# Four edits in the backward half of an H3 convolution and gated MLP kernel: late transposes, an eviction moved to VectorE, two more banks, earlier weights

## The chip, the cores and the metric

The kernel runs on one core of one Trainium2 chip. Its time is the device time of one execution, in microseconds (us). The core has TensorE (PE; PEld is its weight load), VectorE (DVE), ScalarE (ACT), GpSimd (POOL) and SyncE (SP). SP, ACT and POOL also issue the DMA transfers, each from a queue of its own, in order.

## The reference

The reference computes one forward pass and all its gradients for a sequence of 2048 positions and 1024 channels.

```python
xn = layernorm(q)                          # 2048 x 1024
ks = shift convolution of k, four taps per channel (shift_k)
kv = ks * v
y  = long causal convolution of kv with ssm_k (2048 taps per channel, by FFT) + kv * ssm_D
s  = xn * y
g  = silu( ((xn @ w_gate) * (xn @ w_up)) @ w_down )      # 3584 inner columns
out = q + s * g
return out, gradients for q, k, v, shift_k, ssm_k, ssm_D, w_gate, w_up, w_down
```

All inputs and outputs are bf16.

## The kernel before, in words

Everything is done in one program, in four stages, each of which TensorE fills with large products while the convolution's work is slipped in between.

1. **Forward products** (to 568 us). `gu_unit` multiplies the normalised input with slabs of w_up and w_gate (L463), writes both results and their product to DRAM (GUTd, HTd). In between a generator, `conv_forward`, does the shift and the long convolution as short Fourier transforms by matmul and products on VectorE.
2. **Down product and gate** (573 to 787 us). `bm_mm` (L813) multiplies with w_down, held in the tiles U0 to U6. `gate` (from L816) forms the output and the gradients that start the backward pass: dbm, its transposed form DBMT (tiles U7 to U10), and dy, stored to DYd. Its pools `mh`, `mi`, `mt` and `mo` are released at the end of the stage, and only then the pool `bw` is made, which holds the transposed weights wdt.
3. **Backward slabs** (793 to 1852 us). There are 14 slabs of 256 inner columns. `load_wdt` brings a slab of w_down transposed by DMA, on SP's queue. `dh_half` loads the stored gate and up values (tile gul, four buffers), forms two products of eight matmuls each (L915, PSUM psdh), which ScalarE evicts to dht (L917), and multiplies gul by dht on VectorE. Its function `turn` then stores gul to DGUTd and transposes it on TensorE through the one PSUM bank `ps_tr` (L930), from which ScalarE copies it to a tile U4, U5 or U6 (L931). `dw_slab` multiplies the stored input with these for the gradients of w_gate and w_up (L938, PSUM psdw, evicted as wb at L942). One half slab `dh_slab_half(sl + 1, 0)` is done ahead of `dw_slab(sl)`. After the 14 slabs `dwd_slab` forms the gradient of w_down (L1007) and, near the end, weights for the last stage are transposed (L997).
4. **Input gradient** (from 1852 us). `dx_part` (L1063) and `ln_backward`.

**When a turn runs.** `defer` puts a turn on a list; each `flush(age)` adds one to the age of all that is listed and runs those of at least that age. `dh_half` flushes once per product, so twice, and `dw_slab` flushes once for each of its eight columns.

**When the convolution's work runs.** `conv_backward` is a generator whose `yield` values are estimates of VectorE's work. `btick(n)` adds to a counter and lets `bpump` run the generator up to the same share of `C_TOTAL`. It does the transforms of dy for the eight blocks of 128 channels (`dy_forward`, the tiles dyx and kvx, PSUM psS and psP from the pool `ps_c3` and psY from `ps_y`, one bank each). Then come 16 units: eight for the gradients of k and v, eight for that of ssm_k. Each unit is a `product` of two spectra A and B on VectorE and a first part of the inverse transform, `inv_dft` (tile W, written back into B); its rest, the `tail`, is run between the steps of the next unit. For ssm_k the tail is `dh_tail`: four times 16 small matmuls from B into psY (L755), which ScalarE scales and writes into the tile ho in order of time (L758). In ho the eight residues of a position lie next to each other, so that one eviction writes values 16 bytes apart. Last come eight `dk_unit`s, for the gradient of k (tile dka, one buffer) and of shift_k: 16 matmuls into psY (L791), of which VectorE takes diagonals (tile dt2, L795).

All small VectorE operations go through a helper at L182, all loads of `ld` through L61 (SP), stores through `st` at L64 (POOL) and `sta` at L67 (ACT). A scheduler orders the instructions of each engine from the program's order and its priorities when the kernel is built; each engine then runs them strictly in that order.

Of the kernel before, what the change touches and what calls it, by code (L numbers as in the profile page):

```python
# [10 lines left out]
ACT = mybir.ActivationFunctionType  # L11
ALU = mybir.AluOpType
AX = mybir.AxisListType
BF16 = mybir.dt.bfloat16
F32 = mybir.dt.float32
# [4 lines left out]
def build_kernel(  # L20
# [11 lines left out]
    nc = tc.nc  # L32
    P = 128
# [4 lines left out]
    DC = D // P  # L38
    NF = F // P
    SLW = 256  # L40
    NSL = F // SLW
    EPS = 1e-5
    WSC = 2.0 / 2048.0
# [14 lines left out]
    V = nc.vector  # L58

    def ld(out, in_):  # L60
        return nc.sync.dma_start(out=out, in_=in_)  # L61

    def st(out, in_):
        return nc.gpsimd.dma_start(out=out, in_=in_)  # L64
# [15 lines left out]
    def pool(name, bufs=1, side=None, space=None):  # L80
        kw = dict(name=name, bufs=bufs, reuse_waits="tile")
        if side:
            kw["side"] = side
        if space is not None:
            kw["space"] = space
        return tc.alloc_tile_pool(**kw)
# [94 lines left out]
    def tt(o, a, b, op):  # L181
        V.tensor_tensor(o, a, b, op)  # L182

    ADD, SUB, MUL = ALU.add, ALU.subtract, ALU.mult
# [36 lines left out]
    FWD4_W = 2 * (2 * 1.5 + 2.8)  # L221
# [48 lines left out]
    PROD_W = 14.0  # L270
# [29 lines left out]
    INV_W = 2.3 + 2.4 + 2.3 + 2.8  # L300

    def gseg(G, r, j, k):
        a = r % 4
        return G[:, 4 * a + 2 * j + (1 - k if a == 3 else k), :]
# [74 lines left out]
    ps_y = pool("ps_y", 1, space=PSUM)  # L379
# [63 lines left out]
    def defer(fn):  # L443
        later.append([0, fn])

    def flush(age=0):

        for e in later:
            e[0] += 1
        while later and later[0][0] >= age:  # L450
            later.pop(0)[1]()
# [166 lines left out]

    ub = pool("ub", 1, side="right")
    U += [ub.tile([P, 4096], BF16, name=f"U{i}") for i in range(4, 11)]  # L620
    mh = pool("mh", 2, side="right")
    mi = pool("mi", 2, side="right")
    mt = pool("mt", 1, side="right")
# [121 lines left out]
    def dh_tail(ds, G, ew):  # L745
        ho = ew.tile([P, 2, P, 8], BF16, name="ho")
        for c in range(2):
            for rq in range(2):
                ps = ps_y.tile([P, 4, P], F32, name="psY")
                for i in range(4):  # L750
                    r = 4 * rq + i
                    n = 0
                    for j in range(2):
                        for k in range(2):
                            nc.tensor.matmul(ps[:, i, :], gseg(G, r, j, k)[:, c * P:(c + 1) * P], TI[:, j, r, k, :],  # L755
                                             start=(n == 0), stop=(n == 3))
                            n += 1
                nc.scalar.activation(ho[:, c].rearrange("p u r -> p r u")[:, 4 * rq:4 * rq + 4], ps[:], ACT.Copy, scale=WSC)  # L758
                yield 0.1
        st(o_dssmk[ds * P:(ds + 1) * P, :], ho[:].rearrange("p c u r -> p (c u r)"))  # L760
        yield 0.1

# [11 lines left out]
    def dk_unit(ds, tiles, ew):  # L774
        dsl = slice(ds * P, (ds + 1) * P)
        kh, dk = tiles
        acc = ew.tile([P, 2, 8, P], BF16, name="dka")
        wb = lambda j: Wbc[:, j:j + 1, dsl].to_broadcast([P, 8, P])
        for c in range(2):
            tt(acc[:, c], dk[:, c, 3:11, :], wb(3), MUL)  # L780
            for j in (2, 1, 0):
                prod = ew.tile([P, 8, P], BF16, name="dkp")
                tt(prod[:], dk[:, c, j:j + 8, :], wb(j), MUL)
                tt(acc[:, c], acc[:, c], prod[:], ADD)
                yield 1.6
            st(o_dk[:, c, :, dsl], acc[:, c])
        ps = ps_y.tile([P, 4, P], F32, name="psY")
        n = 0
        for c in range(2):
            for r in range(8):  # L790
                nc.tensor.matmul(ps[:].rearrange("p a b -> p (a b)"), dk[:, c, r, :],  # L791
                                 kh[:, c, r:r + 4, :].rearrange("p a b -> p (a b)"), start=(n == 0), stop=(n == 15))
                n += 1
        dt_ = ew.tile([P, 4, P], F32, name="dt2")
        tt(dt_[:], ps[:], ident_f[:].unsqueeze(1).to_broadcast([P, 4, P]), MUL)  # L795
        dr_ = ew.tile([P, 4], F32, name="dr2")
        V.tensor_reduce(dr_[:], dt_[:], AX.X, ADD)
        V.tensor_copy(dsko[:, ds, ::-1], dr_[:])
        yield 1.5

    C_TOTAL = 8 * (FWD4_W + 0.8) + 16 * (PROD_W + INV_W) + 8 * 1.4 + 8 * 5.4 + 8 * 0.5 + 8 * 11.2
    bpump, bdrain = make_pump(conv_backward(), C_TOTAL)

    ddo = const.tile([P, 8], BF16, name="ddo")
# [6 lines left out]
    def bm_mm(ps, ht, i, fc):  # L811
        for dh in range(2):
            nc.tensor.matmul(ps[:, dh * 512:(dh + 1) * 512], ht[:, fc, i * P:(i + 1) * P],  # L813
                             WD[fc // 4][:, fc % 4, dh * 512:(dh + 1) * 512], start=(fc == 0), stop=(fc == NF - 1))
# [39 lines left out]
    def load_ht(bp):  # L854
        ht = mh.tile([P, NF, 256], BF16, name="ht")
        ld(ht[:], HTd[:, bp * 256:(bp + 1) * 256].rearrange("(c f) s -> f c s", f=P))
        return ht

    ht = mh.tile([P, NF, 256], BF16, name="ht")
    for j in range(7):  # L860
        if j % 2 == 0:
# [8 lines left out]
        gate(i, pss[i])  # L870
    for bp in range(1, 8):
        ht = load_ht(bp)
        for i in range(2):
            ps = ps_bm.tile([P, D], F32, name="psbm")
            for fc in range(NF):
                bm_mm(ps, ht, i, fc)
                if fc == 14:
                    flush()
            gate(2 * bp + i, ps)
# [4 lines left out]


    XN = [u8(q, a=4) for q in range(4)]
    bw = pool("bw", 2, side="right")
    bg = pool("bg", 2, side="right")
    ps_dh = pool("ps_dh", 2, space=PSUM)
    ps_dw = pool("ps_dw", 2, space=PSUM)  # L890
# [1 line left out]
    ps_c3 = pool("ps_c3", 1, space=PSUM)  # L892
    ps_y = pool("ps_y3", 1, space=PSUM)
    bcnt = [0]
    BT = 0.94 * (NSL * (8 + 16) + 7 * 16.0)

    def btick(n):
        bcnt[0] += n
        bpump(bcnt[0] / BT)

    def load_wdt(sl):
        wdt = bw.tile([P, DC, SLW], BF16, name="wdt")
        nc.sync.dma_start_transpose(out=wdt[:], in_=B_w_down[sl * SLW:(sl + 1) * SLW, :])
        return wdt

    def dh_half(fc, hf, wdt, dgu):

        fi = fc % 2
        gut = bg.tile([P, 2, 1024], BF16, name="gul", bufs=4)
        ld(gut[:], GUTd[fc, :, :, hf * 1024:(hf + 1) * 1024])  # L910
        dht = bg.tile([P, 1024], BF16, name="dht")
        for k in range(2):
            ps = ps_dh.tile([P, 512], F32, name="psdh")
            for dc in range(DC):
                nc.tensor.matmul(ps[:], wdt[:, dc, fi * P:(fi + 1) * P], DBMT[2 * hf + k][:, dc, :],  # L915
                                 start=(dc == 0), stop=(dc == DC - 1))
            nc.scalar.copy(out=dht[:, k * 512:(k + 1) * 512], in_=ps[:])  # L917
            flush(2)
            btick(1)
        dgt = gut  # L920
        with tc.high_priority(60):
            tt(dgt[:], gut[:], dht[:].unsqueeze(1).to_broadcast([P, 2, 1024]), MUL)

        def turn():
            sta(DGUTd[4 * hf:4 * hf + 4, :, :, fc, :].rearrange("b f a s -> f a b s"),
                dgt[:].rearrange("f a (b s) -> f a b s", s=256))
            for a in range(2):
                ps = ps_tr.tile([P, 8, P], BF16, name="tr")
                for i in range(8):
                    nc.tensor.transpose(ps[:, i, :], dgt[:, a, i * P:(i + 1) * P], ident[:])  # L930
                nc.scalar.copy(out=dgu[:, :, a, fi * P:(fi + 1) * P], in_=ps[:])  # L931
        defer(turn)

    def dw_slab(sl, dgus):
        for dc in range(DC):
            ps = ps_dw.tile([P, 2, SLW], F32, name="psdw")
            for b in range(NB):
                nc.tensor.matmul(ps[:].rearrange("p a f -> p (a f)"), XN[b // 4][:, b % 4, dc * P:(dc + 1) * P],  # L938
                                 dgus[b // 8][:, b % 8].rearrange("p a f -> p (a f)"),
                                 start=(b == 0), stop=(b == NB - 1))  # L940
            wb = bg.tile([P, 2, SLW], BF16, name="wb", bufs=4)
            nc.scalar.copy(out=wb[:], in_=ps[:])  # L942
            fs = slice(sl * SLW, (sl + 1) * SLW)
            sta(o_dwg[dc * P:(dc + 1) * P, fs], wb[:, 0, :])
            sta(o_dwu[dc * P:(dc + 1) * P, fs], wb[:, 1, :])
            flush(2)
            btick(2)

    def load_h(sp):
# [1 line left out]
        nc.sync.dma_start_transpose(out=h, in_=HTd[sp * SLW:(sp + 1) * SLW, :])  # L951
        return h

    wdt = load_wdt(0)
    flush()
    def dh_slab_half(sl, hf, wdt):
        dgu = u8(4 + (2 * sl + hf) % 3, "p (b a f) -> p b a f", b=8, a=2)
# [6 lines left out]
    for sl in range(NSL):  # L964
# [13 lines left out]
        wdt = wnext  # L978
# [124 lines left out]
    for bp in range(1, 8):  # L1103
        t = load_dgut(bp)
        for i in range(2):
            ps = ps_x.tile([P, D], F32, name="psx")
# [68 lines left out]
```

## Time and profile before

| | |
|---|---|
| median of three runs | 2256.11 us (2255.44 to 2267.16) |
| profiled execution | 2267.18 us, its span 2265.1 us |
| busy share of the span | TensorE 94%, VectorE 58%, ScalarE 34%, GpSimd 12% |
| granted TensorE clock, mean | 0.984 |
| DMA | 436.92 MB, mean 193 GB/s |

The span runs from the first to the last instruction of the program; 2.1 us of the execution lie outside of it. A matmul's busy time is its time in a pipeline, so that a busy share near 100% does not say that the array is fully used; waits and the granted clock say where time is lost. "A <- B" in the views of waits reads "A waited until B was done".

### The profile page before, as it was taken

The numbers are of one execution on the slowest core, as the hardware profiler recorded it, in microseconds if no ns is written. First come the engines' busy times: TensorE is split into PE (matmuls) and PEld (weight loads), VectorE is DVE, ScalarE is ACT, GpSimd is POOL, SyncE is SP. The second block draws the span as 40 slices with busy tenths as digits, with TensorE's granted clock in tenths as the row PEclk, the third lists the DMA queues.
The fourth block names the chain that finished last, engine by engine and source line by source line (L and its number), as shares of the span: only waits on it lengthen the run. The fifth ranks groups of instructions, "written<-read, shape, count | busy, mean of one in ns | idle before, by whom it ended". The sixth has DMA issues, their size and how long they took to land.

```text
span 2265.1 us, 29905 instructions
## 1 busy us (share of the span) xinstructions
PE 2122.9 (94%) x12128; PEld 1096.0 (48%) x12128; DVE 1311.4 (58%) x1770; ACT 769.3 (34%) x1040; POOL 273.8 (12%) x440
## 2 busy tenths in 40 slices
PE   5899999999899889989999999988998999999997
PEld 3455555555344455544545545444443455444443
DVE  8779898987354555659775676674456202222122
ACT  4433434343233343333333335554411242111111
POOL 3211111111021110011211200000021000000000
PEclk9999999999999999999999999999999999999999
DMA  9646565555977786686886755546688865323221
GB/s 312 232 175 231 190 207 196 189 174 188 323 233 231 246 263 198 167 258 200 251 211 209 226 163 168 177 160 188 138 240 146 235 216 173 135 107 117 103 107 33
DMA packets 386795, 436.92 MB, mean 193 GB/s; under 512 B 120960, under 2 KB 304280, under 8 KB 375520
## 3 DMA queue, kind: packets, MB, share of 16 engines
q1 hardware_dynamic: 227664, 177.23, 27.7%
q0 software_dynamic: 40944, 175.96, 22.5%
q10 hardware_dynamic: 118048, 81.81, 12.4%
q8 instruction: 95, 1.56, 0.3%
q14 instruction: 44, 0.36, 0.0%
HBM read 237.76 MB, written 179.34 MB: 184 GB/s over the span
## 4 chain that ended last, share of the span: by engine, by line
issue 27%; PE 21%; DVE 7%; ACT 4%; DMA 4%; POOL 1%; ACTq 1%; POOLq 0%; DVEq 0%
PE psdw L938 11%; PE psdw L1007 3%; DVE m L182 3%; PE psdh L915 3%; ACT ho L758 2%; ACT U L931 1%; PE tr L930 1%; DVE gul L182 1%; ACTq L67 1%; PE psY L755 1%; PE psY L314 1%; DMA DYFd<-DX 1%; DVE A L182 1%; POOL out_dram L64 1%; DVE W L182 1%
## 5 line engine op out<-in xcount | busy, mean ns | idle before, releaser
L463 PE MATMUL psg<-U,wslab 128*128 128x512 bf16 x1792 | 407.5, 383 | 9.2 <-ACT gut L465 5.6
L938 PE MATMUL psdw<-U,U 128*128 128x512 bf16 x1792 | 408.0, 382 | 1.3 <-ACT wb L942 1.3
L1063 PE MATMUL psx<-U,dgut 128*128 128x512 bf16 x1408 | 308.5, 379 | 0.0
L463 PEld LDWEIGHTS <-wslab 128*128 128x128 bf16 x1792 | 176.3, 99 | 208.4 <-issue 17.2
L1063 PEld LDWEIGHTS <-dgut 128*128 128x128 bf16 x1792 | 174.7, 98 | 208.1
L938 PEld LDWEIGHTS <-U 128*128 128x128 bf16 x1792 | 174.1, 99 | 193.9 <-issue 6.9
L465 ACT CAST gut<-psg 128x512 bf16<-128x512 f32 x224 | 130.9, 585 | 269.7 <-PE psg L463 252.0
L915 PE MATMUL psdh<-U,wdt 128*128 128x512 bf16 x896 | 213.4, 385 | 6.7 <-DMA wdt<-in_B_w_down_dram 6.7
L813 PE MATMUL psbm<-U,ht 128*128 128x512 bf16 x896 | 199.4, 383 | 10.0 <-DMA ht<-HTd 10.0
L1007 PE MATMUL psdw<-U,U 128*128 128x512 bf16 x896 | 201.6, 381 | 0.0
L182 DVE TENSOR_TENSOR m<-A,B 128x1024 bf16<-128x1024 bf16 (+1 forms) x160 | 116.7, 792 | 92.7 <-DMA B<-KFd 72.0
L942 ACT CAST wb<-psdw 128x512 bf16<-128x512 f32 x112 | 66.5, 594 | 249.8 <-PE psdw L938 213.3
L182 DVE TENSOR_TENSOR dxn<-psx,dxna_t 128x1024 f32<-128x1024 f32 x16 | 19.6, 1224 | 220.8 <-PE psx L1063 220.7
L813 PEld LDWEIGHTS <-ht 128*128 128x128 bf16 x896 | 87.8, 99 | 115.0 <-DMA ht<-HTd 11.0
L931 ACT COPY U<-tr 128x1024 bf16<-128x1024 bf16 x112 | 114.2, 1019 | 59.5 <-PE tr L930 38.0
L1007 PEld LDWEIGHTS <-U 128*128 128x128 bf16 x896 | 86.5, 98 | 98.4 <-issue 1.7
L915 PEld LDWEIGHTS <-wdt 128*128 128x128 bf16 x896 | 86.5, 99 | 95.7 <-DMA wdt<-in_B_w_down_dram 7.2
L182 DVE TENSOR_TENSOR W<-W,psP 128x512 f32<-128x512 f32 x128 | 81.6, 683 | 63.7 <-ACT W L214 54.0
L1079 ACT ACTIVATE junk<-dxn 128x1024 bf16<-128x1024 f32 x16 | 16.9, 1057 | 279.8 <-DVE dxn L182 279.8
L917 ACT CAST dht<-psdh 128x512 bf16<-128x512 f32 x112 | 68.8, 615 | 93.0 <-PE psdh L915 70.0
L182 DVE TENSOR_TENSOR gul<-gul,dht 128x2048 bf16<-128x2048 bf16 x56 | 68.4, 1221 | 53.4 <-ACT dht L917 48.1
L930 PE MATMUL tr<-ident,gul 128*128 128x128 bf16 x896 | 69.5, 221 | 26.6 <-ACT U L931 13.1
(220 smaller groups left out, 2520.5 us busy)
## 6 DMA issues: line engine op xcount, KB each, us to landing
gul<-GUTd SPq DMA_DIRECT2D x56, 512.0 KB, 5.9
DGUTd<-gul ACTq DMA_DIRECT2D x56, 512.0 KB, 5.9
dgut<-DGUTd SPq DMA_DIRECT2D x16, 1792.0 KB, 8.3
GUTd<-gut ACTq DMA_DIRECT2D x48, 512.0 KB, 3.9
A<-DYFd POOLq DMA_DIRECT2D x16, 1024.0 KB, 5.8
out_dram<-wb ACTq DMA_DIRECT2D x224, 64.0 KB, 2.4
ht<-HTd SPq DMA_DIRECT2D x7, 1792.0 KB, 8.3
HTd<-hT POOLq DMA_DIRECT2D x48, 256.0 KB, 3.4
```

The costliest lines, as they stand in the source:

```text
L182: V.tensor_tensor(o, a, b, op)
L463: nc.tensor.matmul(ps[:], w[:, dc, a, fi * P:(fi + 1) * P], XNT[q][:, dc, :], start=(dc == 0), stop=(dc == DC - 1))
L465: nc.scalar.copy(out=gut[:, a, k * 512:(k + 1) * 512], in_=ps[:])
L813: nc.tensor.matmul(ps[:, dh * 512:(dh + 1) * 512], ht[:, fc, i * P:(i + 1) * P], WD[fc // 4][:, fc % 4, dh * 512:(dh + 1) * 512], start=(f ...
L915: nc.tensor.matmul(ps[:], wdt[:, dc, fi * P:(fi + 1) * P], DBMT[2 * hf + k][:, dc, :], start=(dc == 0), stop=(dc == DC - 1))
L917: nc.scalar.copy(out=dht[:, k * 512:(k + 1) * 512], in_=ps[:])
L930: nc.tensor.transpose(ps[:, i, :], dgt[:, a, i * P:(i + 1) * P], ident[:])
L931: nc.scalar.copy(out=dgu[:, :, a, fi * P:(fi + 1) * P], in_=ps[:])
L938: nc.tensor.matmul(ps[:].rearrange("p a f -> p (a f)"), XN[b // 4][:, b % 4, dc * P:(dc + 1) * P], dgus[b // 8][:, b % 8].rearrange("p a f ...
L942: nc.scalar.copy(out=wb[:], in_=ps[:])
L1007: nc.tensor.matmul(ps[:], h[:, b, fi * P:(fi + 1) * P], DBM[b // 4][:, b % 4, dh * 512:(dh + 1) * 512], start=(b == 0), stop=(b == NB - 1))
L1063: nc.tensor.matmul(ps[:, dh * 512:(dh + 1) * 512], t[a][:, 4 * j + f, i * P:(i + 1) * P], WGU[n][:, f, dh * 512:(dh + 1) * 512], start=(n ...
```

## The change

There are four edits and what belongs to them.

- A turn is run once its age is 4 in `dh_half` and 3 in `dw_slab`, in place of 2 in both.
- The eviction of psY into ho is a VectorE operation in place of a ScalarE activation. The work that `dh_tail` announces to the pump rises with it, and `C_TOTAL` too.
- `dk_unit` takes psS and psP from `ps_c3` in turn in place of psY, and dka has two buffers.
- The pool `bw` is made ahead of the pools of the second stage, and the first slab of wdt is loaded in that stage's loop (at bp == 5). The pump does nothing for the first eight ticks of the slabs, and its share is counted from there.

```diff
     ub = pool("ub", 1, side="right")
     U += [ub.tile([P, 4096], BF16, name=f"U{i}") for i in range(4, 11)]
+    bw = pool("bw", 2, side="right")
...
-                nc.scalar.activation(ho[:, c].rearrange("p u r -> p r u")[:, 4 * rq:4 * rq + 4], ps[:], ACT.Copy, scale=WSC)
-                yield 0.1
+                V.tensor_scalar(ho[:, c].rearrange("p u r -> p r u")[:, 4 * rq:4 * rq + 4], ps[:], WSC, None, op0=MUL)
+                yield 0.7
...
-        acc = ew.tile([P, 2, 8, P], BF16, name="dka")
+        acc = ew.tile([P, 2, 8, P], BF16, name="dka", bufs=2)
...
-        ps = ps_y.tile([P, 4, P], F32, name="psY")
+        ps = ps_c3.tile([P, 4, P], F32, name=("psS", "psP")[ds % 2])
...
-    C_TOTAL = 8 * (FWD4_W + 0.8) + 16 * (PROD_W + INV_W) + 8 * 1.4 + 8 * 5.4 + 8 * 0.5 + 8 * 11.2
+    C_TOTAL = 8 * (FWD4_W + 0.8) + 16 * (PROD_W + INV_W) + 8 * 1.4 + 8 * 5.4 + 8 * 2.9 + 8 * 11.2
...
+    def load_wdt(sl):
+        wdt = bw.tile([P, DC, SLW], BF16, name="wdt")
+        nc.sync.dma_start_transpose(out=wdt[:], in_=B_w_down[sl * SLW:(sl + 1) * SLW, :])
+        return wdt
...
         ht = load_ht(bp)
+        if bp == 5:
+            wdt = load_wdt(0)
...
-    bw = pool("bw", 2, side="right")
...
-        bpump(bcnt[0] / BT)
-
-    def load_wdt(sl):
-        wdt = bw.tile([P, DC, SLW], BF16, name="wdt")
-        nc.sync.dma_start_transpose(out=wdt[:], in_=B_w_down[sl * SLW:(sl + 1) * SLW, :])
-        return wdt
+        bpump((bcnt[0] - 8) / (BT - 8))
...
             nc.scalar.copy(out=dht[:, k * 512:(k + 1) * 512], in_=ps[:])
-            flush(2)
+            flush(4)
             btick(1)
...
             sta(o_dwu[dc * P:(dc + 1) * P, fs], wb[:, 1, :])
-            flush(2)
+            flush(3)
             btick(2)
...
-    wdt = load_wdt(0)
     flush()
```

## The prediction

> **What bounds the kernel now.** I read the page's engine line first, then its slices, then the waits of TensorE stretch by stretch, because a sum over the whole span hides which engine is late where.
>
> ```profile
> PE 2122.9 (94%) x12128; PEld 1096.0 (48%) x12128; DVE 1311.4 (58%) x1770; ACT 769.3 (34%) x1040; POOL 273.8 (12%) x440
> PEclk9999999999999999999999999999999999999999
> ```
>
> TensorE is busy 94% of the span and no other engine passes 58%, so time goes away only where TensorE stands idle or runs below its clock. The change leaves its 12128 matmuls and transposes as they are. The next view is TensorE's waits from 787 to 1580 us (the slabs of the gate, up and inner gradients), then from 1580 to 1850 us (the down gradient). Columns: who waited, for whom, total us, times, longest.
>
> ```profile
> PE psY L755 <- ACT ho L758: 14.7, 8, 5.8
> PE tr L930 <- ACT U L931: 13.1, 11, 3.7
> PE tr L930 <- DVE gul L182: 11.6, 5, 4.6
> PE psdh L915 <- DMA wdt<-in_B_w_down_dram: 6.7, 1, 6.7
> PE psY L646 <- DMA dyx<-DYd: 3.7, 1, 3.7
> ...
> PE psY L791 <- DVE dt L182: 6.7, 2, 6.2
> PE psY L755 <- ACT ho L758: 5.1, 3, 1.8
> PE tr L997 <- DMA wn<-in_B_w_up_dram: 4.8, 1, 4.8
> PE psY L791 <- DMA dkh<-DKSHd: 2.7, 1, 2.7
> ```
>
> Each of the four edits is aimed at a line of this list. Their cost is more than the waits, since the clock drops after the long ones. The table by stretches has, near its end, the granted clock; these rows surround the waits for wdt, for two gul products, for ho and for dt.
>
> ```profile
> 790.00:800.00 10.00, 6.37 (x25) 2.97 (x26) 4.82 (x8) 1.61 (x3) 3.60 (x6) 0.66 1.06 303
> 1000.00:1060.00 60.00, 55.36 (x316) 28.82 (x317) 54.77 (x60) 21.29 (x31) 8.53 (x13) 0.94 0.71 205
> 1540.00:1560.00 20.00, 13.92 (x94) 7.93 (x92) 18.54 (x24) 9.21 (x8) 0.00 (x0) 0.83 0.58 206
> 1645.00:1660.00 15.00, 12.27 (x50) 5.07 (x49) 8.29 (x14) 1.17 (x2) 5.01 (x9) 0.89 1.08 313
> 1735.00:1755.00 20.00, 13.81 (x53) 5.64 (x52) 16.04 (x26) 1.17 (x2) 4.75 (x7) 0.83 0.62 160
> ```
>
> Length times the missing share is the time lost: 3.4, 3.6, 3.4, 1.7 and 3.4 us.
>
> [...] a wait of 6.7 us is followed by the 0.66 above, and waits of 1.8 us are followed by nothing. [...] The tile ho is written 16 bytes apart, and there ScalarE takes 2452 ns for 128x512, against 586 ns for the packed yl of the same size: [...] no row shows VectorE writing so. [...] the nearest row, DX<-W at 128x512 out of f32, is 685 ns. I use 685.
>
> ```profile
> L758 ACT ACTIVATE ho<-psY x32: 2433/2452/2524, 1361.9 to 1641.0; 128x512 bf16<-128x512 f32 x32
> L732 ACT CAST yl<-psY x32: 585/586/606, 1021.6 to 1335.9; 128x512 bf16<-128x512 f32 x32
> L182 DVE TENSOR_TENSOR DX<-W 128x512 bf16<-128x512 f32 x64 | 40.2, 685 | 3.5 <-DMA DYFd<-DX 3.5
> ```
>
> **The change part by part.**
>
> *Early down weights.* Where instructions stand I take from the order of the changed program as it is built, which holds no times. There both first transposes of w_down, slabs 0 and 1, stand on SP directly behind the last weight slabs and ahead of the first load into U, so they are issued near 493 us and not at 786.9. Being issued that early, they are moved past every load of the middle stage. They now wait for the last KSHd store (443.7) and the last kv product (446.1), both done. SP issues nothing from 493 to 532 us, where its next load waits for TensorE, and the two took 6.4 us to issue: that stretch hides them. Were it gone, the U loads would be 6.4 us later and TensorE would start L813 that much later. Gone are the 6.7 us wait and 3.4 us of clock. The gul loads, which stood behind the transposes on SP (793.5), follow the U loads near 782 to 787. What is late next: dyx is read after DYd of the last gate is stored (issued 792.0) and landed at 805.3, while the new order has TensorE there near 802; I count 1 us of gain. Sum 11, between 6 and 14.
>
> *Transposes four products late.* A turn now stands 4 products (4 x 1.72 us) behind its own product instead of 2, so a late gul may be 3.4 us later for free; the longest of the five waits is 4.6. Gain 11.6, and 3.6 of clock. The 13.1 us on U are another matter: there is one transpose bank, and the second transpose stands 5 matmuls (1.08 us) behind the first while the copy takes 1.02 and its latency; two of the eleven, 6.7 us, came while ScalarE was held up issuing wb stores for 6.4 and 2.6 us. I expect 3 us back here, as ScalarE loses the ho work. New: the second turn of a half slab comes right ahead of the column that reads it. The order leaves 2.1 to 2.4 us from its last transpose to that read, and copy plus latency need about 1.3, more if ScalarE is in a dht eviction (0.6). 14 slabs by 0.2 us is 3, between 0 and 10. gul has four buffers and three are now held at once; the next load has the 27 us of a dw_slab to land, so nothing. Sum 11.6 + 3.6 + 3 - 3 = 15, between 5 and 20.
>
> *ho by VectorE.* Removed: 14.7 + 5.1 = 19.8 us and 3.4 of clock. Added: 32 x 0.685 = 22 us on VectorE, which is idle over a third of 1280 to 1580 us. Its order decides, for psY has one bank: a group of 16 transposing matmuls can't start before the previous ho is out, and in the new order ho stands behind parts of the next unit's inverse. Walked for one unit from the durations of the trace: last psY of the old unit at 0; B lands 7 us later; product and turn 12.4 + 1.3; W 2.3, B 2.4, W 2.3, B 1.2, then ho at 29.0. TensorE, without waits, has the first psY group done at 23.8 and wants the second at 27.3; it starts at 29.9 and waits 2.6. Walked so, the eight units wait about 2, 3.7, 2.4, 2.5, 2.6, 3.1, 1.5 and 0.6: 18 us, of which I take 16, for groups that move past one another. [...] At 2452 ns instead of 685, 1.8 us more for each unit, 14, and 9 of clock. Sum 19.8 + 3.4 - 16 - 3.4 = 4, between -19 and +23. What queues behind a waiting ho on VectorE are the next product and gul, the first of which waits for B anyhow.
>
> *Two banks for the shift product.* psS and psP lie idle by then. The 6.7 us behind dt go, with 3.4 of clock. The order has 52 instead of 36 matmuls (3.4 us) ahead of the first shift product, which covers the 2.7 us for dkh and 1.7 of clock. Sum 14, between 9 and 15. The second dka buffer ends 26.8 us of VectorE's waits for stores, off the path: nothing.
>
> *Pacing.* The side work starts 8 ticks later, runs 5% faster per tick (647.2 / 413.1 against 628 / 421.1) and ends on the same tick; VectorE keeps a slack of some 4 us per unit. Nothing, at worst -4.
>
> Together 11 + 15 + 4 + 14 = 44. The profiled execution took 2267.2 us, so 2223 by this sum. The median of the three runs is 2256.1, 11 below it; some of the waits above must be missing there, so I take 40 off the median: **2216 us**.
>
> **The rivals.**
>
> *Slow scattered writes.* VectorE pays as ScalarE does. For: the same addresses. Against: nothing shown. 23 us of the gain go: 2239, still faster.
>
> *The transposes change their waiter.* The one transpose bank and ScalarE's stalled issues, not gul, end every wait at L930, and the late copies cost their 10; the ho waits reach 18 to 25. For: ACT U has the largest count. Against: the five gul waits are separate lines. The turn is -5, ho -10, so 11 - 5 - 10 + 14 = 10 off: 2246 to 2252, no measurable change.
>
> *VectorE becomes the bound.* If each of the 24 later psY groups finds a half inverse (2.3 + 2.4) ahead of its ho, and ho costs 2.45, with 3.45 us of products between groups, each waits 3.7: 88 us. Less 20 saved there and 40 elsewhere it is 28 slower, 2284, and up to 41 more if each drops the clock, 2325. It decides from 2.5 us per group. For: one bank and a queue in order. Against: VectorE waits for B 72 us in this part, and the walk finds only one long wait per unit.
>
> **How the numbers follow.** Forecast 60%, slow writes 19%, changed waiter 10%, VectorE the bound 11%. A measurement of this kernel tells about 0.5%, 11 us, from no change: faster 0.79, same 0.10, slower 0.11. The low end takes most of the good bounds of ho, turns and start (19 + 5 + 3 more), 24: 2192. The high end takes in slow writes and the third case: 2254. Left out are the fourth case and a little below the low end.
>
> **What would show it.** Right: no wait of TensorE for wdt; clock 1.00 after 790; no wait of L930 for gul over 1 us; none for dt; ho on VectorE near 0.7 us; waits of psY for ho of 2 to 4 us, one per unit. Wrong: ho near 2.4 us; waits of psY that sum over 40 us; waits of L938 for U at each slab.

## The result, and the profile after

The changed kernel is slower: 2286.13 us median of four runs (2283.51 to 2297.08) against 2256.07 us, a ratio of 1.0131 with a 95% interval of 1.0085 to 1.0177. The profiled execution took 2297.08 us, its span 2295.2 us, which is 30.1 us more than the span before. The mean granted clock fell from 0.984 to 0.977 of full speed; the missing shares times the spans are 36 and 53 us, so by this estimate up to 17 of the 30 us are clock and at least 13 are waits. TensorE's busy time, for the same matmuls, grew by 8.9 us (2131.8 against 2122.9) and its idle time by 21, which puts less on the clock and more on the waits.

The first two lines are the engine line and TensorE's clock row of the page.

```profile
PE 2131.8 (93%) x12128; PEld 1097.0 (48%) x12128; DVE 1387.5 (60%) x1802; ACT 694.2 (30%) x1008; POOL 273.6 (12%) x440
PEclk9999999999999999999999999999999899999999
```

VectorE has 76 us more to do and ScalarE 75 us less. The 32 operations that moved are as long on the one engine as on the other, 2432 ns on VectorE against 2452 on ScalarE. This row is from the view of the tile ho in the changed kernel (shortest, middle and longest in ns, then first and last start in us):

```profile
L759 DVE TENSOR_SCALAR ho<-psY x32: 2409/2432/2449, 1363.9 to 1664.8; 128x512 bf16<-128x512 f32 x32
```

TensorE's waits (total us, times, longest), first from 787 to 1580 us, then from 1580 to 1880 us:

```profile
PE psY L756 <- DVE ho L759: 23.0, 8, 6.8
PE psdw L940 <- ACT U L933: 9.0, 2, 7.8
PE psdh L917 <- ACT dht L919: 6.7, 3, 5.9
PE psS L201 <- ACT W L214: 6.5, 1, 6.5
PE psY L314 <- ACT yl L733: 5.8, 2, 4.9
PE tr L932 <- ACT U L933: 2.3, 5, 0.8
...
PE psS L792 <- DMA dkh<-DKSHd: 12.3, 3, 8.4
PE psY L756 <- DVE ho L759: 10.6, 5, 3.3
PE tr L998 <- DMA wn<-in_B_w_up_dram: 10.1, 1, 10.1
```

Three of the lines that the change was aimed at are gone: no wait for wdt, none of L932 for gul, none for dt. The fourth, the wait for ho, grew from 19.8 to 33.6 us. The wait for dkh, which the two banks were to cover, grew from 2.7 to 12.3, and other lines are new. These rows of the table by stretches surround them (the three last columns: granted clock, DMA share, GB/s):

```profile
790.00:800.00 10.00, 9.35 (x50) 4.36 (x49) 8.08 (x11) 5.02 (x8) 2.53 (x4) 1.00 1.04 384
1040.00:1060.00 20.00, 14.09 (x59) 6.22 (x57) 15.81 (x16) 4.28 (x8) 7.46 (x11) 0.83 0.90 248
1165.00:1195.00 30.00, 22.17 (x140) 11.51 (x138) 28.02 (x30) 9.39 (x13) 7.06 (x11) 0.89 0.99 255
1525.00:1545.00 20.00, 13.18 (x76) 6.94 (x74) 16.15 (x12) 1.17 (x2) 0.53 (x1) 0.83 0.21 70
1700.00:1710.00 10.00, 7.07 (x33) 3.04 (x31) 0.00 (x0) 1.76 (x3) 0.00 (x0) 1.00 1.27 88
1710.00:1720.00 10.00, 4.58 (x11) 1.60 (x12) 3.52 (x6) 0.00 (x0) 0.00 (x0) 0.53 1.19 189
1815.00:1835.00 20.00, 9.81 (x59) 5.01 (x58) 0.00 (x0) 5.09 (x6) 0.00 (x0) 0.71 0.94 285
```

The first row is the edit that worked: full clock where 0.66 stood before. The others are new or larger losses. From 1700 to 1720 us VectorE and GpSimd are all but idle and the DMA engines are busy all the time, at first for 88 GB/s: VectorE, and then TensorE, wait for transfers. Measured by first starts, the slabs begin 4.2 us earlier than before (789.4 against 793.6), the products of w_down's gradient (L1008) start 14.5 us later (1595.1 against 1580.6) and the last stage (L1064) starts 30.1 us later (1882.6 against 1852.5).

Several chains lie behind the new lines. Two of them run through ScalarE's queue. These lines are ScalarE's own waits from 900 to 1200 us:

```profile
ACT dht L919 <- DVE gul L182: 21.0, 3, 8.1
ACT W L214 <- DVE DX L182: 15.0, 4, 9.6
ACT U L933 <- DVE m L182: 11.3, 2, 9.8
```

A turn begins with the store of gul, which ScalarE issues. With the turn run late, TensorE no longer waits for a late gul, but this store does, and dht and yl stand behind it in ScalarE's queue. So at 1052 and 1110 us TensorE waits 5.9 us for dht and 4.9 for yl: the wait for gul has changed its name. The wait of 7.8 us for U at 1184 us is of another kind. There gul was done, but the issue of its store alone held ScalarE's queue for 7.7 us, where the median of the 56 is 0.59 (start, us, queue, operation):

```profile
1175.98 7.72 ACTq L67 DMA_DIRECT2D DGUTd<-gul  x1
```

The 6.5 us for W go back to a store of DX that was issued at 952.5 us and took 18.1 us to land, with no transposing load under way.

The last chain, for dkh, is in the timeline of the changed kernel (start, us, queue, operation; in brackets the idle time before and what ended it):

```profile
1689.07 33.51 SPq L953 DMA_TRANSPOSE U<-HTd  x2
1692.51 0.54 POOL L64 DMA_DIRECT2D dkh<-DKSHd  x1 [2.64 <-DVE dkp L182]
1694.48 0.63 POOL L64 DMA_DIRECT2D dkh<-DKSHd  x1
...
1715.42 1.03 PE L792 MATMUL psS<-kh,dkh 128*128 128x512 bf16 x2 [8.35 <-DMA dkh<-DKSHd]
```

The load of dkh was issued 3.4 us behind a transposing load of HTd, and came 22.9 us later. The kernel before has such meetings too: behind transposing loads, five transfers issued from 1159 to 1162 us and seven from 1708 to 1720 us took 14 to 18 us. The view of the tile dkh gives the shortest, middle and longest landing of its 16 loads in the changed kernel:

```profile
DMA to landing us min/median/max: 5.9/7.4/23.0
```

### The profile page after: what moved, and what is told of

It reads as the page before. It is cut to its first block, busy times and chain, and to the rows that moved or that the text cites. A ratio compares the mean times of both kernels' runs of the same rounds, so it can differ in the third digit from the quotient of the medians.

```text
span 2295.2 us, 29877 instructions
## 1 busy us (share of the span) xinstructions
PE 2131.8 (93%) x12128; PEld 1097.0 (48%) x12128; DVE 1387.5 (60%) x1802; ACT 694.2 (30%) x1008; POOL 273.6 (12%) x440
## 4 chain that ended last, share of the span: by engine, by line
issue 35%; PE 15%; DVE 11%; DMA 6%; POOL 3%; ACT 2%; ACTq 0%; POOLq 0%; DVEq 0%
PE psdw L940 8%; DVE m L182 4%; PE psdh L917 3%; DVE W L182 2%; DVE ho L759 1%; DMA B<-KFd 1%; POOL out_dram L64 1%; DVE A L182 1%; DMA B<-HFd 1%; DVE gul L182 1%; ACT U L933 1%; PE psY L756 1%; PE psdw L1008 1%; PE tr L932 1%; DMA DYFd<-DX 1%
## 5 line engine op out<-in xcount | busy, mean ns | idle before, releaser
L940 PE MATMUL psdw<-U,U 128*128 128x512 bf16 x1792 | 419.1, 385 | 9.0 <-ACT U L933 9.0
L1064 PE MATMUL psx<-U,dgut 128*128 128x512 bf16 x1408 | 308.5, 379 | 0.0
L1064 PEld LDWEIGHTS <-dgut 128*128 128x128 bf16 x1792 | 174.8, 98 | 208.1
L940 PEld LDWEIGHTS <-U 128*128 128x128 bf16 x1792 | 174.3, 99 | 198.6 <-issue 21.5
L917 PE MATMUL psdh<-U,wdt 128*128 128x512 bf16 x896 | 209.6, 385 | 7.8 <-ACT dht L919 6.7
L1008 PE MATMUL psdw<-U,U 128*128 128x512 bf16 x896 | 202.8, 382 | 0.0
L944 ACT CAST wb<-psdw 128x512 bf16<-128x512 f32 x112 | 65.7, 586 | 289.2 <-PE psdw L940 275.7
L182 DVE TENSOR_TENSOR dxn<-psx,dxna_t 128x1024 f32<-128x1024 f32 x16 | 19.6, 1225 | 220.5 <-PE psx L1064 220.4
L917 PEld LDWEIGHTS <-wdt 128*128 128x128 bf16 x896 | 87.3, 99 | 104.0 <-issue 13.4
L1008 PEld LDWEIGHTS <-U 128*128 128x128 bf16 x896 | 86.8, 99 | 98.8 <-issue 2.5
L759 DVE TENSOR_SCALAR ho<-psY 128x512 bf16<-128x512 f32 x32 | 77.8, 2430 | 48.1 <-PE psY L756 46.0
L1080 ACT ACTIVATE junk<-dxn 128x1024 bf16<-128x1024 f32 x16 | 16.9, 1057 | 279.5 <-DVE dxn L182 279.5
L1011 ACT CAST wb<-psdw 128x512 bf16<-128x512 f32 x56 | 32.8, 586 | 204.4 <-PE psdw L1008 197.4
```

What stands on the lines that cost most here:

```text
L759: V.tensor_scalar(ho[:, c].rearrange("p u r -> p r u")[:, 4 * rq:4 * rq + 4], ps[:], WSC, None, op0=MUL)
L1008: nc.tensor.matmul(ps[:], h[:, b, fi * P:(fi + 1) * P], DBM[b // 4][:, b % 4, dh * 512:(dh + 1) * 512], start=(b == 0), stop=(b == NB - 1))
L1064: nc.tensor.matmul(ps[:, dh * 512:(dh + 1) * 512], t[a][:, 4 * j + f, i * P:(i + 1) * P], WGU[n][:, f, dh * 512:(dh + 1) * 512], start=(n ...
```

## The experiments

The kernel before was run beside every set on the same chip; its median there lay between 2261.8 and 2266.2 us, so kernels are compared by their ratio to it. The changed kernel itself was run in the first set only, four times against four, so its 1.0131 is the least certain ratio here. Theory S says that the length of the write of ho on VectorE makes the loss. Its rivals are T (the late turns, through ScalarE's queue) and L (the two banks and the last units). Later come D and P (the move meets the banks, or the pump's idle ticks), V (it meets nothing), M (late side work costs) and X and F (transposing loads, and their phase). In the diffs, + is the experiment and - the kernel that it starts from.

### ho back on ScalarE

```diff
-                V.tensor_scalar(ho[:, c].rearrange("p u r -> p r u")[:, 4 * rq:4 * rq + 4], ps[:], WSC, None, op0=MUL)
-                yield 0.7
+                nc.scalar.activation(ho[:, c].rearrange("p u r -> p r u")[:, 4 * rq:4 * rq + 4], ps[:], ACT.Copy, scale=WSC)
+                yield 0.1
...
-    C_TOTAL = 8 * (FWD4_W + 0.8) + 16 * (PROD_W + INV_W) + 8 * 1.4 + 8 * 5.4 + 8 * 2.9 + 8 * 11.2
+    C_TOTAL = 8 * (FWD4_W + 0.8) + 16 * (PROD_W + INV_W) + 8 * 1.4 + 8 * 5.4 + 8 * 0.5 + 8 * 11.2
```

> The changed kernel with ho written by ScalarE again (and its pump weight as before); the late turns, the two banks and the early weights stay. Theory S (the write of ho takes 2.43 us on VectorE too, stands there in an in-order queue ahead of products, gul and dk work, and this is what costs the time): 2225 to 2245 us, TensorE's wait for ho falls from 33.6 back to 15 to 20 us, the start of L1008 comes before 1580. Theory T (a turn four products late puts its DGUTd store, and so a wait for gul, into ScalarE's queue ahead of dht, yl and the U copies, and this is the loss): 2270 to 2285, and waits for ACT dht, yl, U of 20 us remain. Theory L (the last units: loads of dkh and wn late because of the second dka buffer and the psS/psP banks): 2270 to 2285, and the waits of 8 and 10 us at L792 and L998 remain.

Measured: 2244.18 us, ratio 0.9913 (0.9893 to 0.9932). L1008 starts at 1570.1, and TensorE's wait for ho, from 570 us on, is

```profile
PE psY L756 <- ACT ho L759: 19.3, 15, 2.3
```

S holds and T and L fall as main causes: the other three edits are a gain of 0.9%, and the moved eviction takes that and 1.3% more.

### The turns early again

```diff
-            flush(4)
+            flush(2)
...
-            flush(3)
+            flush(2)
```

> The changed kernel with the turns at ages 2 and 2 again, all else as changed. Theory S: 2270 to 2300, within 15 us of the changed kernel's 2286, since the turns were worth little either way. Theory T: 2250 to 2262, the waits for ACT dht, yl and U that follow a DVE gul are gone from 1040 to 1180 us. Theory L: 2275 to 2290.

Measured: 2288.83 us, 1.0098 (1.0072 to 1.0124), no difference from the changed kernel that the intervals can tell. T falls. TensorE's waits from 900 to 1200 us in this kernel:

```profile
PE tr L932 <- DVE gul L182: 29.2, 4, 16.9
```

Here the wait for gul is back under its old name, and larger. The longest, 16.9 us, is for a gul that stands on VectorE behind a product, and this product waits from 1044 us on for A. The line is from VectorE's waits around that time:

```profile
DVE m L182 <- DMA A<-DYFd: 18.5, 1, 18.5
```

A was issued 0.4 us behind the transposing load of w_down (1039.08 and 1038.72 us). The load of A took 23.0 us; the loads of A have a median of 6.1 in this kernel.

### ho written side by side

The order in time of the gradient of ssm_k is left out; all else stays.

```diff
-                V.tensor_scalar(ho[:, c].rearrange("p u r -> p r u")[:, 4 * rq:4 * rq + 4], ps[:], WSC, None, op0=MUL)
+                V.tensor_scalar(ho[:, c].rearrange("p u r -> p (u r)")[:, 512 * rq:512 * rq + 512], ps[:].rearrange("p a b -> p (a b)"), WSC, None, op0=MUL)
```

> The changed kernel with VectorE writing ho packed, 512 values side by side: the order in time of the gradient of ssm_k is left out, all else stays, the same instructions on the same engines. Theory S: one ho takes 0.65 to 0.70 us in place of 2.43, the wait for ho falls from 33.6 to 15 to 22 us, the time to 2235 to 2260. If the place in VectorE's queue and not the length of the write were the cause, ho is short and the wait stays at 28 to 34 us, 2270 to 2286. Theory T and Theory L: 2275 to 2290.

Measured: 2243.61 us, 0.9913 (0.9883 to 0.9943). The group of ho (busy us, mean ns of one, then VectorE's idle time before it), and below it TensorE's wait from 1280 to 1850 us:

```profile
L759 DVE TENSOR_SCALAR ho<-psY 128x512 bf16<-128x512 f32 x32 | 22.1, 689 | 62.6 <-PE psY L756 61.3 <-DMA out_dram<-ho 1.3
```

```profile
PE psY L756 <- DVE ho L759: 12.2, 6, 4.6
```

The same instruction of the same size takes 689 ns, not 2430, and the whole of the loss against ScalarE's version is gone (0.9913 both). The wait for ho, 12.2 us, is even below the 15 that were expected at least. In this kernel the place in VectorE's queue is not at fault, the addresses are. Nor is what ho announces to the pump, which is as in the changed kernel. The trace shows one more stall of 20.9 us of VectorE at 1049 us, again with A issued 0.5 us behind a transposing load (it landed at 1069.6 us; the view of waits itself names no cause).

### The eviction on VectorE alone

```diff
-                nc.scalar.activation(ho[:, c].rearrange("p u r -> p r u")[:, 4 * rq:4 * rq + 4], ps[:], ACT.Copy, scale=WSC)
-                yield 0.1
+                V.tensor_scalar(ho[:, c].rearrange("p u r -> p r u")[:, 4 * rq:4 * rq + 4], ps[:], WSC, None, op0=MUL)
+                yield 0.7
...
-    C_TOTAL = 8 * (FWD4_W + 0.8) + 16 * (PROD_W + INV_W) + 8 * 1.4 + 8 * 5.4 + 8 * 0.5 + 8 * 11.2
+    C_TOTAL = 8 * (FWD4_W + 0.8) + 16 * (PROD_W + INV_W) + 8 * 1.4 + 8 * 5.4 + 8 * 2.9 + 8 * 11.2
```

(from the kernel before)

> The kernel before with one edit alone: ho by VectorE, with its pump weight. Theory S: 2280 to 2310, slower than before by 25 to 50 us. Theory T and Theory L: 2250 to 2266, as before within 10 us.

Measured: 2275.8 us, 1.0045 (1.0030 to 1.0060). Slower, though less than S said and more than T and L said, and by a fifth of what the same edit costs beside the others (1.0131 / 0.9913 = 1.0220, both intervals combined 1.017 to 1.027). S as stated is too simple: the edit meets something that another edit brings.

### What it meets: the banks or the pump

The two banks undone:

```diff
-        acc = ew.tile([P, 2, 8, P], BF16, name="dka", bufs=2)
+        acc = ew.tile([P, 2, 8, P], BF16, name="dka")
...
-        ps = ps_c3.tile([P, 4, P], F32, name=("psS", "psP")[ds % 2])
+        ps = ps_y.tile([P, 4, P], F32, name="psY")
```

> The changed kernel with the two banks undone (the shift product in psY again, one dka buffer); ho on VectorE, late turns, early weights stay. What is to be told: alone the VectorE ho cost 0.45% (ratio 1.0045), beside the other edits 2.2% (0.9913 to 1.0131). Theory D (it meets the two banks: the dk units come late behind ho, their dkh loads then sit 15 to 20 us among the transposing loads, and psS waits 8.5 to 15 us): ratio 1.000 to 1.006, no wait at L792 over 4 us. Theory P (it meets the pump's eight idle ticks, which put all of the side work later): 1.012 to 1.020, the banks' gain lost on top. Theory V (no meeting, simply more work in VectorE's queue): 1.012 to 1.020.

The pump counted from the first tick:

```diff
-        bpump((bcnt[0] - 8) / (BT - 8))
+        bpump(bcnt[0] / BT)
```

> The changed kernel with the pump counted from the first tick again, not from the ninth; all else as changed. Theory P: ratio 0.998 to 1.005, the last psY of ho before 1645 in place of 1664.8. Theory D and theory V: 1.008 to 1.016.

Measured: without the banks 2290.76 us, 1.0147 (1.0119 to 1.0176); with the pump from the first tick 2257.52 us, 0.9989 (0.9970 to 1.0007). The banks are not what it meets, the eight idle ticks are: 1.4% (1.0131 / 0.9989 = 1.0142, 1.009 to 1.019), some 32 us, from an edit that moves the side work by a few products. But the reason that theory P gave, late side work, does not carry the loss. The first and last start of ho with the pump from the first tick:

```profile
L759 DVE TENSOR_SCALAR ho<-psY x32: 2410/2434/2440, 1341.9 to 1645.8; 128x512 bf16<-128x512 f32 x32
```

The last ho starts 19 us earlier, but most of this is the loss itself: L1008 starts at 1579.7 us here and at 1595.1 with eight ticks. Counted from the start of L1008, the last ho comes after 66.2, 69.7 and 71.7 us with no, eight and 16 idle ticks. So the ticks do put the side work later, by a few microseconds, but the time does not follow: with 16 ticks (below) it is shorter than with eight.

### The other edits, with ho on ScalarE

The diffs are those of the sections above, put together: ho on ScalarE and early turns; ho on ScalarE and the banks undone; ho on ScalarE and the pump from the first tick. The last has only the early weights on the kernel before:

```diff
+    bw = pool("bw", 2, side="right")
...
+        if bp == 5:
+            wdt = load_wdt(0)
...
-    bw = pool("bw", 2, side="right")
...
-    wdt = load_wdt(0)
```

> ho by ScalarE again and the turns at ages 2 and 2 again: what is left is the two banks and the early weights. If the late turns were worth their predicted 15 us: ratio 0.9975 to 0.999. If they are worth nothing, as the pair of the changed kernel and its twin with early turns says (1.0131 and 1.0098): 0.990 to 0.993.

> ho by ScalarE again and the two banks undone: what is left is the late turns and the early weights. If the two banks were worth their predicted 14 us (the 6.7 us behind dt, 2.7 for dkh, two drops of the clock): ratio 0.996 to 0.999, a wait for dt of 3 to 7 us at L792. If they are worth nothing: 0.990 to 0.993.

> The changed kernel with ho by ScalarE and the pump counted from the first tick: two banks, late turns, early weights. If the idle ticks cost by themselves: ratio 0.980 to 0.988. If they cost only where VectorE is loaded with ho (0.9989 against 1.0131 there): 0.989 to 0.993, the same as with the idle ticks (0.9913).

> The kernel before with one edit alone: the pool bw made early and the first slab of wdt loaded in the second stage; the pump is not touched. The prediction's 11 us: ratio 0.994 to 0.996, no wait for wdt. If this edit is all of the gain that is left without the VectorE ho (0.9913 to 0.9927 in three kernels): 0.991 to 0.994.

Measured, against 0.9913 with all of them:

| | ratio | interval |
|---|---|---|
| without the late turns | 0.9927 | 0.9900 to 0.9954 |
| without the two banks | 0.9922 | 0.9901 to 0.9943 |
| without the idle ticks | 0.9946 | 0.9926 to 0.9966 |
| early weights alone, on the kernel before | 0.9983 | 0.9966 to 1.0000 |

Neither the late turns nor the banks can be told from nothing. The early weights bring 0.17% alone, some 4 us, less than both expected ranges had. The idle ticks, which cost 1.4% with ho on VectorE, gain 0.3% here, which neither range had. The traces say where the wait for gul goes: with early turns and ho on ScalarE, L932 waits 7.5 us for gul and 23.1 for U from 787 to 1580 us; with late turns it waits 5.8 us for U and none for gul, but L940 waits 9.0 for U and L917 5.4 for dht. Of 30.6 us, 20.2 stay. Of the banks' gain: without them L792 waits 4.4 us for dt and L998 4.7 for wn; with them there is no wait for dt, and L998 waits 7.2 for wn.

### Transposing loads

All 28 replaced by plain loads of the same bytes, with ho on VectorE and on ScalarE (that transposition is left out in both):

```diff
-        nc.sync.dma_start_transpose(out=h, in_=HTd[sp * SLW:(sp + 1) * SLW, :])
+        nc.sync.dma_start(out=h.rearrange("p b f -> p (b f)"), in_=HTd[sp * SLW:(sp + 1) * SLW, :].rearrange("(p a) s -> p (a s)", a=2))
...
-        nc.sync.dma_start_transpose(out=wdt[:], in_=B_w_down[sl * SLW:(sl + 1) * SLW, :])
+        nc.sync.dma_start(out=wdt[:].rearrange("p c f -> p (c f)"), in_=B_w_down[sl * SLW:(sl + 1) * SLW, :].rearrange("(p a) d -> p (a d)", a=2))
```

> The changed kernel with the 28 transposing loads (w_down into wdt, HTd into U) replaced by plain loads of the same bytes: the transposition of both is left out, so their products are of other numbers. Theory X (the loss is made by transposing loads: a transfer that is issued within a microsecond or so behind one takes 15 to 28 us in place of 6, and the changed kernel's phase puts dkh and gul stores there at 1164, 1669 and 1689): the waits at L792 for dkh and at L998 shrink to under 4 us, no transfer takes over 14 us in the slabs, and against its twin with ho on ScalarE the loss falls from 2.2% to under 1%. Theory V (VectorE's queue alone): the difference between the twins stays at 1.8 to 2.4%.

> The twin: the same plain loads (transposition left out), with ho by ScalarE. It serves the comparison above. Both theories: ratio 0.975 to 0.992, no slower than with transposing loads (0.9913).

Measured: 2267.01 us, 0.9997 (0.9983 to 1.0012), and 2244.12 us, 0.9896 (0.9874 to 0.9918). The pair stands at 0.9997 / 0.9896 = 1.0102 (1.0075 to 1.0129), not at 1.0220: with eight idle ticks about half of what the VectorE ho costs goes away with the transposing loads. The loads of HTd, with transposing loads (the changed kernel) and with plain ones:

```profile
DMA to landing us min/median/max: 6.7/10.5/32.2
```

```profile
DMA to landing us min/median/max: 4.8/6.7/10.9
```

The longest dkh load is 10.5 us with plain loads, not 23.0, and TensorE's waits from 1580 us on are

```profile
PE psY L756 <- DVE ho L759: 10.7, 5, 4.8
PE tr L998 <- DMA wn<-in_B_w_up_dram: 7.2, 2, 5.3
PE psS L792 <- DMA dkh<-DKSHd: 0.7, 1, 0.7
```

Three points of theory X missed: the pair differs by 1.02% and not by less than 1%, L998 still waits 5.3 us, and the wait for W, which a slow store of DX made in the changed kernel, is 7.3 us and not 6.5 in a kernel that has no transposing load at all. What the replacement takes away is two things, since a transposing load of HTd also holds SP's queue for a median of 5.9 us (4.2 to 20.7) at its issue, a plain one for 0.32. The two were not separated. Nor was the shift of phase that any such edit brings: plain loads were run with eight idle ticks only.

The loads of HTd alone:

```diff
-        nc.sync.dma_start_transpose(out=h, in_=HTd[sp * SLW:(sp + 1) * SLW, :])
+        nc.sync.dma_start(out=h.rearrange("p b f -> p (b f)"), in_=HTd[sp * SLW:(sp + 1) * SLW, :].rearrange("(p a) s -> p (a s)", a=2))
```

> The changed kernel with the 14 transposing loads of HTd alone replaced by plain loads of the same bytes (that transposition is left out); w_down is still transposed. Both together gave 0.9997 against 1.0131. Theory E (the cost lies at the end, where dkh and dka meet the HTd loads: 8.5 us at L792, 10.3 at L998 and the half clock behind them): 1.000 to 1.004. Theory W (it lies in the slabs, at 1164, where gul stores meet the w_down load: 8 us at L940, 5 at L314): 1.009 to 1.013.

Measured: 2279.29 us, 1.0056 (1.0035 to 1.0076), between the two theories. The ratios would put 0.75% at the end and 0.6% in the slabs, but the traces don't bear that out. Against the changed kernel both stages are 13 us shorter: the slabs take 792.4 and not 805.7 us, the gradient of w_down 274.1 and not 287.4. Yet the slabs' gain lies between 1090 and 1190 us, and the first load of HTd is issued at 1529. The stall at 1184 us is missing there without a cause in the edit. Executions of this kernel lie between 2261.0 and 2289.3 us, so such meetings seem to come and go from one execution to the next.

### More and fewer idle ticks

```diff
-        bpump((bcnt[0] - 8) / (BT - 8))
+        bpump((bcnt[0] - 4) / (BT - 4))
```

and the same with 16, with ho on VectorE and on ScalarE.

> The changed kernel with 4 idle ticks of the pump in place of 8 (ho on VectorE). With none it stands at 0.9989, with 8 at 1.0131. Theory M (late side work is what costs, the more the later): 1.003 to 1.009. Theory F (it is a matter of phase: which side loads, gul stores and dkh loads fall behind a transposing load, and a step of 4 ticks shuffles that): anywhere from 0.996 to 1.016, and the time follows the transfers that take over 20 us in the dw and dwd slabs.

> The changed kernel with 16 idle ticks (ho on VectorE). Theory M: 1.020 to 1.035. Theory F: 0.996 to 1.018, no worse than with 8 by more than the noise.

> The changed kernel with ho by ScalarE and 16 idle ticks: 0.9946 with none, 0.9913 with 8. Theory M: 0.992 to 1.000. Theory F: 0.987 to 0.997; if the gain from 0 to 8 was the dy_forward start being no longer late for dyx (3.6 to 4.9 us), 0.989 to 0.993 again.

Measured:

| idle ticks | ho on VectorE | ho on ScalarE |
|---|---|---|
| 0 | 0.9989 (0.9970 to 1.0007) | 0.9946 (0.9926 to 0.9966) |
| 4 | 0.9954 (0.9933 to 0.9974) | not run |
| 8 | 1.0131 (1.0085 to 1.0177) | 0.9913 (0.9893 to 0.9932) |
| 16 | 1.0047 (1.0023 to 1.0070) | 0.9965 (0.9938 to 0.9993) |

M falls on the left, where the time neither rises nor falls with the ticks; on the right both ranges hold the one result. F fits, but that proves little, since its ranges were wide; with four ticks the ratio even lies just below its 0.996. TensorE's waits say more. In the left column the wait for ho is 22.6, 27.9, 33.6 and 30.0 us, while the wait of L792 for dkh is none, 0.4, 12.3 and 12.9: the two slow settings are those in which dkh is late. The longest known dkh load is 8.3, 8.7, 23.0 and 17.7 us. On the right, 16 ticks have a dkh load of 19.6 us and 8.8 us of waits for dkh, at a ratio of 0.9965 and not 0.9913. Late dkh alone is too short for the whole difference: 12.3 us of some 32.

### Two banks for ho

```diff
-                ps = ps_y.tile([P, 4, P], F32, name="psY")
+                ps = ps_c3.tile([P, 4, P], F32, name=("psS", "psP")[rq])
```

in `dh_tail`, with ho on ScalarE and on VectorE.

> A candidate: the changed kernel with ho by ScalarE again, and the matmuls of ho in psS and psP in turn in place of psY, since these two banks lie idle until the dk units. Its twin with one bank stands at 0.9913, with 15 waits for ho of 19.3 us. If the waits for ho are real losses: no wait for ho over 1 us, ratio 0.980 to 0.987. If they are only passed on to the next wait (VectorE's inverse, or U): 0.989 to 0.993.

> The changed kernel, ho by VectorE, with the matmuls of ho in psS and psP in turn. It stands at 1.0131 with one bank and waits 33.6 us for ho. If the one bank makes the loss (TensorE held at the second group until VectorE has come to the first): the wait falls under 12 us, ratio 0.994 to 1.002. If VectorE's 76 us of added work and the phase make it: 1.004 to 1.014.

Measured: 2225.83 us, 0.9817 (0.9784 to 0.9850), and 2260.04 us, 0.9976 (0.9955 to 0.9997). The wait for ho stayed a little above what was expected in both (1.8 us once, and 12.5 in all), the ratios lie within the ranges for a real loss. The first beats both kernels: 1.8% less than before, 3.1% less than the changed one (0.9817 / 1.0131 = 0.969, 0.964 to 0.975). TensorE's waits from 1280 us on in the first, then in the second:

```profile
PE tr L932 <- ACT U L933: 8.0, 7, 2.2
PE tr L998 <- DMA wn<-in_B_w_up_dram: 7.7, 2, 6.5
PE psdw L940 <- ACT wb L944: 2.2, 1, 2.2
PE psdh L917 <- ACT dht L919: 2.2, 3, 0.9
PE psS L756 <- ACT ho L759: 1.8, 1, 1.8
```

```profile
PE tr L998 <- DMA wn<-in_B_w_up_dram: 11.5, 2, 10.4
PE psS L756 <- DVE ho L759: 8.9, 4, 5.3
PE psS L792 <- DMA dkh<-DKSHd: 3.7, 1, 3.7
PE psP L756 <- DVE ho L759: 3.6, 2, 2.3
```

The wait for ho, 19.3 us with one bank, came from the single bank: psY held TensorE until ScalarE's 2.45 us were over, 15 times. With two banks the eviction lies beside products on ScalarE, with 1.8 us of waits left. On VectorE it still leaves 12.5 us.

## Why the prediction was wrong

The prediction took 40 us off the median; the changed kernel takes 30 us more. Three of its steps failed: the price of ho, the pacing at nothing, and the gains of the other edits, counted as sure. By its own steps:

| step | predicted | measured |
|---|---|---|
| early down weights | -11 | -4 alone (0.9983; the interval reaches from -8 to 0) |
| late turns | -15 | about 0 (0.9913 against 0.9927; on VectorE 1.0131 against 1.0098) |
| two banks | -14 | about 0 (0.9913 against 0.9922; on VectorE 1.0131 against 1.0147) |
| these and the idle ticks together | -40 | -20 (0.9913) |
| ho by VectorE | -4, bad end +19 | +10 alone, +50 in the changed kernel (1.0045; 1.0220) |
| pacing | 0, at worst +4 | -7 with ho on ScalarE, +32 with ho on VectorE |

The last two rows overlap and are not to be added. Without the idle ticks the move of ho costs 0.4% (0.9989 against 0.9946), without the move the ticks gain 0.3%; some 1.8%, or 40 us, appear only where both meet (1.0131 x 0.9946 / (0.9989 x 0.9913) = 1.0176).

**The price of ho.** This is the step that turned the sign in the runs: the changed kernel stands at 1.0131, and at 0.9913 with ho written side by side. In the prediction's own sum a slow write takes only 23 us, so that sum would have stayed on the side of a gain. I took 685 ns from a row of the same size (DX<-W) against 2452 ns from a row with the same addresses, because no row showed VectorE writing so. It takes 2432 ns. The kernel before shows the price of scattered writes on ScalarE alone (2452 ns, and 586 for the packed yl), and I took it for that engine's. VectorE pays it as well: 2430 ns scattered and 689 ns side by side, in two kernels that differ in nothing else. So 685 ns is the price of the packed form.

**The walk came close, its use did not.** The waits that it gave were 16 us at 685 ns and 30 us at 2452 ns. Measured were 12.2 and 33.6 us (23.0 + 10.6), though in 13 waits of up to 6.8 us and not one per unit. The clock in its sum, 3.4 us for two waits and 9 more at 2452 ns, was my estimate: 1.7 us a wait, as around the wait of 2.7 us for dkh (1645 to 1660 us) in the kernel before. From which length on a wait costs clock was not shown: in the changed kernel the clock is 0.66 from 1410 to 1415 us, behind a wait for ho of 2.9 us, and 1.00 from 1615 to 1630, around one of 3.3. At the waits of 6.8 and 5.6 us it is 0.66 from 1535 to 1545 and 0.77 from 1560 to 1575; the missing shares come to some 8.5 us at the 13 waits. With plain loads the move costs 1.0%, some 23 us, near the bad end of 19. What the walk left out is that a later ho moves the side work and its loads behind it; that this shift is what costs the rest fits the runs, but is not shown by itself.

**Pacing at nothing.** I counted the idle ticks by VectorE's slack alone. But they cost 1.4% beside the move. As far as the traces show, they shift which loads are issued while a transposing load is under way. Where A, dkh or a store of gul was slow there, it took 14 to 25 us (A 25.0 in the packed kernel, dkh 23.0 and the stores of gul 14.1 to 20.4 in the changed one) against medians of 5.5, 7.4 and 7.0, and VectorE, ScalarE's queue and TensorE waited one after the other, with a clock of 0.53 after it (at 1710 us). Why eight ticks are worse than four or 16 stays open.

**Gains passed on.** The late turns and the banks removed their waits, as predicted: no L932 for gul, no L792 for dt. They brought next to nothing. Other waits stand in their place: U and dht in ScalarE's queue, and wn at the end. With the early weights alone the slabs begin 5.4 us earlier (788.2 against 793.6) and there is no wait for wdt, but L1008 starts 3.4 us later (1584.0 against 1580.6), with 28.8 us of waits for ho in that execution, one of 14.7. The next waits that I had named, U one column early and dkh covered by 16 more matmuls, were not these.

**The rivals.** "VectorE becomes the bound" had the number, 2284 to 2325, but not the mechanism: it wanted 24 waits of 3.7 us, 88 in all, and there are 13 of 33.6 us in all. "Slow scattered writes" had the mechanism and gave 2239, since it took the other 40 us for sure. "The transposes change their waiter" was right on the turns: on ScalarE's version 20.2 of 30.6 us stay, in part under other names. It had ScalarE's stalled issues as the cause; in the changed kernel one such issue (7.7 us) makes the longest wait for U, while the waits for dht and yl come from the store's place in that queue.

**What stays open.** With eight ticks the move of ho costs 2.2%, with plain loads 1.0%, and with no ticks and the transposing loads in place 0.4%. So the loss beyond some 1% goes with either change. Whether plain loads help as such, by freeing SP's queue, or by shifting the phase is not shown. Slow landings have another source as well: in the kernel before, four transfers issued from 949 to 956 us took 16 to 20 us, while the last transposing load had landed at 947.0 and the next was issued at 996.8. Waits and landings were read from one profiled execution of each kernel, and with no, four and 16 ticks only 14 of the 16 landings of dkh are in the trace.

## What to carry to other kernels

Take an instruction's price from a row with the same addresses, not from one of the same size: here an eviction that writes 16 bytes apart took as long on VectorE (2432 ns) as on ScalarE (2452). Where TensorE waits for an eviction out of a single bank, try a second bank before moving the eviction; here that was 1.0% (0.9817 against 0.9913), and the move was a loss of 0.4 to 2.3% in each of the eight pairs that differ in it. When a wait is removed, find who stands behind it in the same queue. When side work is shifted beside other transfers, try several shifts: here four of them lay between 0.9954 and 1.0131 in no order.

## What the runs showed of the hardware

- VectorE and ScalarE pay about the same for a 128x512 write with values 16 bytes apart: 2432 against 689 ns, and 2452 against 586 ns (the packed yl), 3.4 and 3.6 ns more for each value of a partition.
- The transposing loads of HTd landed after 10.5 us (median) and 32.2 at most, the same bytes loaded plainly after 6.7 and 10.9. In the kernel before they took 9.4 and 25.8.
- Of the transfers that the changed kernel issued from 787 to 1890 us while a transposing load was under way, 23 of 127 took over 14 us to land (median 7.6 us); of the other 491, five did (median 4.5). In the kernel before it is 13 of 124 and five of 497. From 1700 to 1710 us the DMA engines were busy all the time and moved 88 GB/s. Which holds up which is not shown. The dkh load that GpSimd issued at 1692.5 us landed at 1715.4, 5.9 us before the transposing load that SP had issued at 1689.1 (1721.3): it did not have to wait until that load had landed.
